# Leaving out a DMA that reads one element of each row of w_in ahead of its load

## The chip, the cores and the metric

The kernel runs on one core of a Trainium2 chip. The metric is the device time of one execution in microseconds (us), as the median of several runs. A core has five engines that run their own instruction lists in order: TensorE (PE: matmuls, with weight loads shown as PEld), VectorE (DVE), ScalarE (ACT), GpSimd (POOL) and SyncE (SP). ScalarE, SyncE and GpSimd also issue DMA transfers, which 16 DMA engines carry out. A transfer that changes the type (here float32 in memory to float16 on the chip) is issued by GpSimd.

## The reference

Two stages. First an attention over 4 batches, 8 heads, 768 positions and 64 dimensions per head, with a bias by distance, in which each position sees the first 8 positions and the 96 latest ones:

```python
scores = scale * np.matmul(q, k.transpose(0, 1, 3, 2))
keep = is_global | is_local          # pos < 8, or 0 <= rel < 96
scores = np.where(keep, scores + bias, -1e9)
a = softmax(scores)
attn_out = np.matmul(a, v)
```

Its output, as 3072 tokens of 512 numbers, goes through two dense layers:

```python
h = np.maximum(x @ w_in, 0.0)        # w_in: 512 x 2048
out = (h * h) @ w_out                # w_out: 2048 x 512
```

## The kernel before

The 3072 tokens are cut into 24 tiles of 128; 6 tiles make a batch. Attention goes tile by tile: q and k are transposed (tile `trp`, L416, and a copy to `qk` by VectorE, L429), scores are computed against the tile itself and the one before (`sp`, L466), ScalarE takes the exponential (`ex`, L479), VectorE multiplies by a mask that holds bias and reach (`ph`, L485), TensorE multiplies with v (`av`, L495), VectorE divides (`rec`, `tm`, L504 and L505), and the result is transposed (`trx`, L511) into `xt`. From tile 6 on the transposes are done by DMA, issued by SyncE. `fix_k` and `fix_v` copy the first 32 positions of a batch from tile to tile.

The dense layers work on chunks of tiles, eight chunks of one tile and then eight of two. Layer 1 (`first`, L639) makes `hps` from `w_in_sb` and `xt` in 16 blocks of 128 of d_ff, with 4 matmuls for each block and chunk; ScalarE applies the maximum (`hr`, L647) and VectorE squares (`h`, L654). Layer 2 (`second`, L660) makes `yps` from `w_out_sb` and `h`, VectorE copies it, and SyncE stores it.

w_in is loaded in four quarters of 512 columns (`load_w_in`, L395), each with all 512 rows; w_out in four quarters of 512 rows (`load_w_out`, L402). All these loads, and those of q, k and v from tile 1 on (and v of tile 0), are issued by GpSimd in one written order (L728): v of tile 0; q, k, v of tiles 1 and 2; the first quarter of w_in; q, k, v of tile 3; the other three quarters of w_in; the four of w_out; then tiles 4 and up. q and k of tile 0 come by another way, as float32 in two halves each (`load_early`, L374): q on SyncE's queue, k on ScalarE's. Ahead of the k halves stands `touch_w_in` (L391): a DMA that reads the first element of each of w_in's 512 rows into a small tile that nothing uses.

The order of the rest is not written out: the class `Plan` makes it while the program is built. Each piece of work is added with an estimate of its length, with what it needs and makes, with buffers that it takes and frees, and a rank. `emit` then walks in planned time, picks for each engine what can start first, and by rank among those, and appends it to that engine's list. DMA transfers have an amount of work and share the DMA engines in the plan; a landing of GpSimd's loads comes later by `late(at)` nanoseconds, depending on the planned time. Where TensorE is planned to idle before 45 us, `idle` puts in matmuls on a blank tile (`warm`, L269), one for every 220 ns of the gap; their results are not used. What the chip does then follows the lists, and semaphores between engines, whatever the plan's times were. A change of an estimate or the loss of one DMA can therefore change the lists of all engines.

Of the kernel before, what the change touches and what calls it, by code (L numbers as in the profile page):

```python
# [8 lines left out]
FP32 = mybir.dt.float32  # L9
# [4 lines left out]
P = 128  # L14


class Dma:
# [5 lines left out]
    def add(self, at, queue, work, item):  # L23
        self.coming.append((at, queue, work, item))
        self.coming.sort(key=lambda x: x[0])
# [26 lines left out]
class Plan:  # L52
# [115 lines left out]
                gone[key] = done  # L168

    def late(self, at):  # L170
        return 700 if at < 15500 else 1300 if at < 43000 else 0


SURE = {"PE": 0, "ACT": 60, "DVE": 60}
# [4 lines left out]
def kernel(  # L179
# [11 lines left out]
    nc = tc.nc  # L191
# [3 lines left out]
    d_model, d_ff = moe_w_in.shape  # L195
    NT = S // P
    NPAIR = H // 2
    NFT = d_ff // P
    NCT = d_model // P
# [12 lines left out]

    NUDGE = {('attention', 11): -10, ('attention', 1): 10, ('attention', 13): -10, ('attention', 7): 100, ('layer 2', 1): 25, ('layer 2', 6): 100, ('attention', 8): 10, ('layer 2', 11): -100, ('attention', 3): 10, ('layer 1', 9): -100, (3.5, 1): 100, ('attention', 20): -25, (2.5, 2): 200, (2, 9): -100, ('attention', 6): 10, (4.5, 16): 25, ('layer 2', 13): -200, ('attention', 23): -200, (1.5, 4): -25, ('layer 1', 5): -10, ('layer 1', 10): -10, ('attention', 5): -200, (4, 16): -100, ('layer 2', 0): 50, ('attention', 19): -10, (2, 4): 25, ('attention', 14): 200, ('attention', 9): 50, ('layer 1', 1): 100, (2, 15): -10, (6, 11): -10, ('attention', 18): -10, ('layer 2', 15): 10, ('attention', 2): -100, ('layer 1', 0): 50, (1.5, 8): 100, (3, 3): 200, ('layer 1', 11): -50, (6, 4): 10, ('layer 1', 2): -25, ('layer 2', 8): 50, ('attention', 10): 25, (1.5, 9): 100, (4.5, 4): -10, ('layer 1', 8): 10, (4.5, 7): 100, ('layer 1', 14): 100, ('layer 1', 13): -25}

    EARLY_QK, TOUCH = ("SP","ACT"), "ACT"

    EARLY_V = None

    W_IN = 4


    ADDED = 0
# [11 lines left out]
    const = ctx.enter_context(tc.tile_pool(name="const", bufs=1))  # L234
# [18 lines left out]

    mask = const.tile([P, 3, 2, NPAIR, P], FP16, name="mask")
    w_in_sb = const.tile([P, NCT, d_ff], FP16, name="w_in_sb")
    touched = const.tile([P, NCT, 1], FP32, name="touched")
    w_out_sb = const.tile([P, NFT, d_model], FP16, name="w_out_sb")


# [14 lines left out]
    add = plan.op  # L274
    vec = nc.vector
    live = {}

    def pool_dma(ns, fn, work, **how):
        add("POOL", ns, fn, work=work, to=914, back=850, **how)
# [42 lines left out]
    def constants():  # L322
        add("DVE", 120, lambda: vec.memset(blank, 0.0), rank=-999)
        add("DVE", 250, lambda: vec.tensor_scalar(
            out=ident, in0=dist[:, 0:P], scalar1=0.0, scalar2=None, op0=ALU.is_equal),
            needs=["dist"], makes=["ident"], rank=-999)
        if EARLY:
            add("DVE", 250, lambda: vec.tensor_scalar(
                out=ident32, in0=dist[:, 0:P], scalar1=0.0, scalar2=None, op0=ALU.is_equal),
                needs=["dist"], makes=["ident32"], rank=-998)  # L330
        add("DVE", 2350, fill_reach, needs=["dist"], makes=["reach"], rank=-997)
        if ADDED:
            for h in range(H):
                add("ACT", 190, lambda h=h: fill_diag(h), needs=["ident"], makes=[("diag", h)],
                    rank=-990 + h)
        for h in range(H):
            add("ACT", 420, lambda h=h: fill_mask(h), needs=["reach"], makes=[("mask", h)],
                rank=-990 + h if h < 4 else -185)
# [22 lines left out]
    def fetch(t, names="qkv"):  # L361
        for name in names:
            pool_dma(876, lambda name=name: load(t, name), 851, makes=[("s" + name, t)],
                     takes=[("stage", ("stage", t))] if name == "q" else
                     [("v", ("v", t))] if name == "v" else [],
                     needs=["ones"] if name == "v" else [])
# [20 lines left out]
            needs=["ev", "ones"], makes=[("sv", 0)], takes=[("v", ("v", 0))], rank=-100)  # L387


    def touch_w_in():  # L390
        {"ACT": nc.scalar, "SP": nc.sync}[TOUCH].dma_start(out=touched, in_=moe_w_in[:, 0:1].rearrange("(k p) f -> p k f", p=P))  # L391

    def load_w_in(c):
        n = d_ff // W_IN
        pool_dma(745, lambda: nc.gpsimd.dma_start(  # L395
            out=w_in_sb[:, :, c * n:(c + 1) * n],
            in_=moe_w_in[:, c * n:(c + 1) * n].rearrange("(k p) f -> p k f", p=P)),
            10240 // W_IN if W_IN == 4 else 1340, makes=[("w_in", c)])

    def load_w_out(c):  # L400
        n = NFT // 4
# [124 lines left out]
    def all_of(name, t):  # L526
        return [(name, t, p) for p in parts_of(t)]
# [95 lines left out]
    def banks(t0):  # L623
        return 1 if t0 < 12 else 2

    def home(t0):
        return "one" if t0 in (0,) else "big"

    def first(c, t0, n, m):
        per = 4 // n  # L630
        if m == 0:
            live["h2", c] = buf("h2", [P, NFT * 2 * P], FP16, "h2")[:, 0:NFT * n * P].rearrange(
                "p (m c) -> p m c", m=NFT)
        i, place = divmod(m, banks(t0) * per)
        if place == 0:
            live["hps", c, i] = buf(home(t0), [P, banks(t0), 512], FP32, "hps")
        w, o = divmod(place, per)
        for kk in range(NCT):
            nc.tensor.matmul(live["hps", c, i][:, w, o * n * P:(o + 1) * n * P],  # L639
                             lhsT=w_in_sb[:, kk, m * P:(m + 1) * P],  # L640
                             rhs=live["xt", c][:, kk, 0:n * P],
                             start=kk == 0, stop=kk == NCT - 1)

    def relu(c, t0, n, i):
        live["hr", c, i] = hr = buf("hr", [P, 2, 512], FP16, "hr")
        w, x = 4 // n * n * P, banks(t0)
        nc.scalar.activation(out=hr[:, 0:x, 0:w], in_=live["hps", c, i][:, 0:x, 0:w], func=AF.Relu)  # L647

    def square(c, t0, n, i):
        per, x = 4 // n, banks(t0)  # L650
        hr = live["hr", c, i][:, 0:x, 0:per * n * P]
        to = live["h2", c][:, x * per * i:x * per * (i + 1), :].rearrange(
            "p (x m) c -> p x (m c)", x=x)
        vec.tensor_tensor(out=to, in0=hr, in1=hr, op=ALU.mult)  # L654
# [17 lines left out]
    def layer_1(c, t0, n, due):  # L672
        xs = [y for t in range(t0, t0 + n) for y in all_of("x", t)]
        per, x = 4 // n, banks(t0)
        for m in range(NFT):
            i, place = divmod(m, x * per)
            add("PE", 4 * (n * 54 + 1), lambda m=m: first(c, t0, n, m),
                needs=xs + [("w_in", m * W_IN // NFT)] + ([("l1", c, m - 1)] if m else []),
                makes=[("l1", c, m)],
                takes=([(home(t0), ("hps", c, i))] if place == 0 else [])  # L680
                + ([("h2", ("h2", c))] if m == 0 else []),
                frees=[("xt", c)] if m == NFT - 1 else [], rank=due(m))
            if place == x * per - 1:
                cols = x * per * n * P
                add("ACT", 70 + 84 * cols // 100, lambda i=i: relu(c, t0, n, i),
                    needs=[("l1", c, m)], makes=[("hr", c, i)], frees=[("hps", c, i)],
                    takes=[("hr", ("hr", c, i))], rank=due(m))
                add("DVE", 90 + 52 * cols // 100, lambda i=i: square(c, t0, n, i),
                    needs=[("hr", c, i)], makes=[("h2", c, y) for y in range(
                        x * per * i, x * per * (i + 1))], frees=[("hr", c, i)], rank=due(m))  # L690
# [25 lines left out]
    with tc.manual_schedule():  # L716
        for names, t in []:
            fetch(t, names)
        add("POOL", 470, iota, makes=["dist"])
        constants()  # L720
        add("DVE", 300, ones, makes=["ones"], rank=-995)
        if EARLY:
            fetch_early()
        if EARLY_V:
            fetch_early_v()
        if TOUCH:
            add(TOUCH, 530, touch_w_in, rank=-1000, work=460, to=210, back=1000)
        for kind, n in [('v', 0), ('qkv', 1), ('qkv', 2), ('i', 0), ('qkv', 3), ('i', 1), ('i', 2), ('i', 3), ('o', 0), ('o', 1), ('o', 2), ('o', 3), ('qkv', 4), ('qkv', 5), ('qkv', 6), ('qkv', 7), ('qkv', 8), ('qkv', 9), ('qkv', 10), ('qkv', 11), ('qkv', 12), ('qkv', 13), ('qkv', 14), ('qkv', 15), ('qkv', 16), ('qkv', 17), ('qkv', 18), ('qkv', 19), ('qkv', 20), ('qkv', 21), ('qkv', 22), ('qkv', 23)]:  # L728
            if kind in "io":
                {"i": load_w_in, "o": load_w_out}[kind](n)  # L730
            else:
                fetch(n, kind)
        t0 = 0
        for c, n in enumerate(CHUNKS):
            for j in range(n):
                attention(t0 + j, c, j, n, lambda st, t0=t0, j=j, n=n:
                          100 * (t0 - n + j) + 6 * st - 100
                          + NUDGE.get(("attention", t0 + j), 0) + NUDGE.get((st, t0 + j), 0))
            layer_1(c, t0, n, lambda m, t0=t0, n=n, c=c: 100 * (t0 + n * m / NFT)
                    + NUDGE.get(("layer 1", c), 0))  # L740
            layer_2(c, t0, n, lambda j, part, t0=t0, n=n, c=c: 100 * (t0 + n + j + part / 4)
                    + 150 + NUDGE.get(("layer 2", c), 0))
            t0 += n
        plan.emit()
# [35 lines left out]
```

## Time and profile before

| | |
|---|---|
| Median of 3 runs | 215.76 us (215.57 to 215.81) |
| The profiled execution's own time | 214.87 us |
| Its span | 213.1 us |
| TensorE busy | 205.6 us, 96% of the span |
| VectorE, ScalarE, GpSimd busy | 122.1, 102.7, 68.1 us |
| Layer 1, layer 2 matmuls | 91.7 and 91.2 us busy |
| Granted TensorE clock | 0.998 |

The span is the part of one execution that the profiler saw from the first to the last instruction; the execution's own time lies 1.77 us above it. In the chain, every line is a stretch of work that released the next one, back from the end. In the timeline, the first number is the start, the second the length, and what stands in square brackets is the idle time before it, with what ended it. A DMA's landing is counted from its issue.

### The profile page before, as it was taken

The page shows a single profiled execution, that of the slowest core. Times are in us where ns is not written, and L with a number is a line of the kernel's source. Part 1 is how long each engine was busy: PE and PEld are TensorE (multiplying, and loading weights), DVE is VectorE, ACT ScalarE, POOL GpSimd, SP SyncE. Part 2 cuts the span into 40 slices and gives each one's busy share as a digit, 9 for nine tenths or more (in the row PEclk, how much of TensorE's full clock was granted, in tenths as well). Part 3 has the DMA queues.
Part 4 walks back from the last instruction along what each step waited for, and adds up shares of the span by engine and source line. Part 5 has one row for each costly group of instructions (what it writes and reads, how often), then busy time and mean ns, then how long its engine had stood idle before and what let it go on. Part 6 is the DMA issues. An engine that isn't in the chain of part 4 may idle for free.

```text
span 213.1 us, 5399 instructions
## 1 busy us (share of the span) xinstructions
PE 205.6 (96%) x2253; PEld 145.6 (68%) x2253; DVE 122.1 (57%) x296; ACT 102.7 (48%) x132; POOL 68.1 (32%) x84
## 2 busy tenths in 40 slices
PE   7869999999999999999999999999999999999994
PEld 4458986657967665875878585757676574888453
DVE  5697562774647877657566545664646674232321
ACT  4775663433764656565464635453353641345100
POOL 8975433727604544632207230451000000000000
PEclk9999999999999999999999999999999999999999
DMA  8999999999996999999939999699511222100112
GB/s 121 150 174 205 207 207 173 182 150 253 154 166 127 163 185 203 183 136 205 173 67 98 137 127 134 115 148 179 105 25 52 77 69 82 49 0 3 49 49 98
DMA packets 112232, 27.61 MB, mean 130 GB/s; under 512 B 104784, under 2 KB 109264, under 8 KB 112208
## 3 DMA queue, kind: packets, MB, share of 16 engines
q0 software_dynamic: 77024, 13.37, 87.3%
q1 hardware_dynamic: 33600, 13.64, 30.7%
q10 hardware_dynamic: 1584, 0.26, 0.7%
q8 instruction: 17, 0.28, 0.5%
q14 instruction: 7, 0.06, 0.1%
HBM read 27.27 MB, written 6.29 MB: 157 GB/s over the span
## 4 chain that ended last, share of the span: by engine, by line
PE 90%; DMA 4%; POOL 3%; DVE 1%; issue 0%
PE yps L660 40%; PE hps L639 39%; PE sp L466 5%; PE av L495 5%; DMA w_in_sb<-in_moe_w_in_dram 4%; POOL s L359 2%; POOL v L359 1%; PE trp L416 1%; PE trx L511 0%; DVE qk L429 0%; DVE tm L505 0%; PE warm L269 0%; DVE rec L504 0%; DVE y L429 0%; DVE v L442 0%
## 5 line engine op out<-in xcount | busy, mean ns | idle before, releaser
L639 PE MATMUL hps<-xt,w_in_sb 128*128 128x128 f16 (+1 forms) x1024 | 91.7, 246 | 1.0 <-DMA w_in_sb<-in_moe_w_in_dram 1.0
L660 PE MATMUL yps<-w_out_sb,h 128*128 128x512 f16 (+2 forms) x416 | 91.2, 363 | 0.0
L639 PEld LDWEIGHTS <-w_in_sb 128*128 128x128 f16 x1024 | 79.2, 98 | 12.7 <-DMA w_in_sb<-in_moe_w_in_dram 1.2
L647 ACT ACTIVATE hr<-hps 128x512 f16<-128x512 f32 (+1 forms) x72 | 52.7, 739 | 68.5 <-PE hps L639 64.9
L660 PEld LDWEIGHTS <-h 128*128 128x128 f16 x416 | 37.0, 98 | 34.8 <-DVE h L654 0.4
L654 DVE TENSOR_TENSOR h<-hr 128x512 f16<-128x512 f16 (+1 forms) x72 | 36.7, 511 | 38.8 <-ACT hr L647 38.6
L479 ACT ACTIVATE ex<-sp 128x1024 f16<-128x1024 f32 (+1 forms) x45 | 42.9, 1002 | 20.0 <-PE sp L466 19.9
L359 POOL DMA_DIRECT2D v<-in_v_dram x24 | 21.5, 896 | 64.1 <-issue 19.7
L485 DVE TENSOR_TENSOR ph<-ex,mask 128x1024 f16<-128x1024 f16 (+1 forms) x45 | 30.0, 676 | 14.1 <-ACT ex L479 13.9
L429 DVE COPY y<-yps 128x512 f32<-128x512 f32 (+2 forms) x26 | 16.9, 648 | 20.0 <-PE yps L660 19.7
L359 POOL DMA_DIRECT2D s<-in_q_dram x23 | 20.5, 891 | 7.9 <-PE hps L639 2.4
L359 POOL DMA_DIRECT2D s<-in_k_dram x23 | 20.7, 898 | 4.6 <-DMA w_out_sb<-in_moe_w_out_dram 2.9
L505 DVE TENSOR_TENSOR tm<-av,rec 128x256 f16<-128x256 f32 x48 | 20.4, 424 | 1.7
L495 PE MATMUL av<-v,ph 128*128 128x65 f16 x352 | 15.0, 193 | 1.0 <-DVE ph L485 1.0
L466 PEld LDWEIGHTS <-qk 64*128 64x128 f16 x352 | 9.9, 94 | 8.7 <-issue 5.9
L495 PEld LDWEIGHTS <-ph 128*128 128x128 f16 x352 | 13.6, 97 | 3.1 <-DVE ph L485 1.4
L466 PE MATMUL sp<-qk 64*128 64x128 f16 x352 | 14.2, 218 | 0.5 <-DVE qk L429 0.2
L504 DVE RECIPROCAL rec<-av 128x4 f32<-128x4 f32 x48 | 8.5, 176 | 9.3 <-PE av L495 9.2
L269 PE MATMUL warm<-blank 128*128 128x256 f16 x37 | 7.7, 317 | 1.2 <-DVE v L345 1.2
L439 DVE COPY qk<-qk 128x128 f16<-128x128 f16 x16 | 4.8, 302 | 1.2 <-PE sp L466 0.6
L427 ACT COPY xt<-trx 128x512 f16<-128x512 f16 (+1 forms) x6 | 3.1, 515 | 4.9 <-PE trx L511 4.9
L269 PEld LDWEIGHTS <-blank 128*128 128x128 f16 x37 | 3.8, 113 | 2.1 <-DVE v L345 1.2
(32 smaller groups left out, 38.1 us busy)
## 6 DMA issues: line engine op xcount, KB each, us to landing
out_dram<-y SPq DMA_DIRECT2D x23, 256.0 KB, 3.4
v<-in_v_dram POOLq DMA_DIRECT2D x24, 128.0 KB, 5.0
s<-in_q_dram POOLq DMA_DIRECT2D x23, 128.0 KB, 5.3
s<-in_k_dram POOLq DMA_DIRECT2D x23, 128.0 KB, 5.9
w_in_sb<-in_moe_w_in_dram POOLq DMA_DIRECT2D x4, 512.0 KB, 10.1
w_out_sb<-in_moe_w_out_dram POOLq DMA_DIRECT2D x4, 512.0 KB, 15.9
qk<-s SPq DMA_TRANSPOSE x18, 6.0
xt<-tm SPq DMA_TRANSPOSE x18, 4.6
```

Of the source, the lines that this page charges most:

```text
L269: nc.tensor.matmul(to[:, 0:2 * P], lhsT=blank[:, 0:P], rhs=blank[:, 0:2 * P], start=True, stop=True)
L359: nc.gpsimd.dma_start(out=dst, in_=source(t, name))
L429: vec.tensor_copy(out=out, in_=src)
L466: nc.tensor.matmul(live["sp", t, before, part][:, e, a, :], lhsT=live["qk", t - before][rows, 1, a, :], rhs=live["qk", t][rows, 0, a, :], ...
L479: nc.scalar.activation(out=some(live["ph" if t < ADDED else "ex", t, before], part), in_=some(live["sp", t, before, part], part), func=AF. ...
L485: vec.tensor_tensor(out=some(live["ph", t, before], part), in0=some(live["ex", t, before], part), in1=some(mask[:, kind], part), op=ALU.mult)
L495: nc.tensor.matmul(av[:, i, :], lhsT=live["ph", t, before][:, h % 2, h // 2, :], rhs=v_bufs[(t - before) % len(v_bufs)][:, h, :], start=be ...
L505: vec.tensor_tensor(out=live["tm", t][:, 4 * g:4 * g + 4, :], in0=av[:, :, 0:D], in1=rec[:, :, None].to_broadcast([P, 4, D]), op=ALU.mult)
L639: nc.tensor.matmul(live["hps", c, i][:, w, o * n * P:(o + 1) * n * P], lhsT=w_in_sb[:, kk, m * P:(m + 1) * P], rhs=live["xt", c][:, kk, 0: ...
L647: nc.scalar.activation(out=hr[:, 0:x, 0:w], in_=live["hps", c, i][:, 0:x, 0:w], func=AF.Relu)
L654: vec.tensor_tensor(out=to, in0=hr, in1=hr, op=ALU.mult)
L660: nc.tensor.matmul(live["y", c, j, cols][:, 0:cols[1] - cols[0]], lhsT=live["h2", c][:, m, j * P:(j + 1) * P], rhs=w_out_sb[:, m, cols[0]: ...
```

## The change

The call of `touch_w_in` falls away, with its tile, so that ScalarE's list begins with the two k halves of tile 0. The function itself is written anew, but with `TOUCH = ()` nothing calls it. The width of w_in's parts is given as a list of four equal ones, which is the same four quarters with the same planned work. And `late` changes: between 11.5 and 15.5 us of planned time, GpSimd's loads are now taken to land 1300 ns late instead of 700. `NUDGE`, which shifts ranks, is unchanged.

```diff
     def late(self, at):
-        return 700 if at < 15500 else 1300 if at < 43000 else 0
+        return 700 if at < 11500 else 1300 if at < 43000 else 0
...
-    EARLY_QK, TOUCH = ("SP","ACT"), "ACT"
+    EARLY_QK = ("SP","ACT")
+    TOUCH = ()
...
-    W_IN = 4
+    W_IN = (4,) * 4
...
-    touched = const.tile([P, NCT, 1], FP32, name="touched")
...
-    def touch_w_in():
-        {"ACT": nc.scalar, "SP": nc.sync}[TOUCH].dma_start(out=touched, in_=moe_w_in[:, 0:1].rearrange("(k p) f -> p k f", p=P))
+    def touch_w_in(queue, behind):
+        to = const.tile([P, NCT, 1], FP32, name="touched")
+        if behind:
+
+            add("DVE", 60, lambda: vec.memset(to, 0.0), needs=behind, makes=["touch"], rank=-1000)
+        add(queue, 530, lambda: {"ACT": nc.scalar, "SP": nc.sync}[queue].dma_start(
+            out=to, in_=moe_w_in[:, 0:1].rearrange("(k p) f -> p k f", p=P)),
+            needs=["touch"] if behind else [], rank=-1000, work=460, to=210, back=1000)
 
     def load_w_in(c):
-        n = d_ff // W_IN
+        at = slice(sum(W_IN[:c]) * P, sum(W_IN[:c + 1]) * P)
         pool_dma(745, lambda: nc.gpsimd.dma_start(
-            out=w_in_sb[:, :, c * n:(c + 1) * n],
-            in_=moe_w_in[:, c * n:(c + 1) * n].rearrange("(k p) f -> p k f", p=P)),
-            10240 // W_IN if W_IN == 4 else 1340, makes=[("w_in", c)])
+            out=w_in_sb[:, :, at], in_=moe_w_in[:, at].rearrange("(k p) f -> p k f", p=P)),
+            200 + 590 * W_IN[c], makes=[("w_in", c)])
...
-                needs=xs + [("w_in", m * W_IN // NFT)] + ([("l1", c, m - 1)] if m else []),
+                needs=xs + [("w_in", [c for c, n in enumerate(W_IN) for _ in range(n)][m])] + ([("l1", c, m - 1)] if m else []),
...
-        if TOUCH:
-            add(TOUCH, 530, touch_w_in, rank=-1000, work=460, to=210, back=1000)
+        for queue, behind in TOUCH:
+            touch_w_in(queue, behind)
```

## The prediction

> **What bounds the kernel now.** I read the engines in stretches of the span first, then the chain that ended last, and then the landings of the loads in the first 30 us. The stretches (columns: length; busy time and instructions of PE, weight loads, DVE, ACT, POOL; granted clock; DMA share; GB/s):
>
> ```profile
> span 213.1 us, 5399 instructions
> 15.28:20.36 5.08, 4.87 (x86) 4.16 (x87) 4.50 (x13) 2.04 (x4) 3.11 (x4) 1.00 1.42 201
> 20.36:60.00 39.64, 39.64 (x547) 30.48 (x548) 22.68 (x54) 20.83 (x32) 19.27 (x22) 1.00 1.82 189
> 60.00:150.00 90.00, 90.00 (x987) 63.04 (x988) 57.30 (x140) 47.71 (x58) 32.45 (x37) 1.00 1.54 150
> 150.00:209.99 59.99, 59.98 (x522) 40.82 (x516) 26.78 (x55) 21.86 (x22) 0.00 (x0) 1.00 0.18 54
> ```
>
> From 20.36 us to 209.99 us TensorE has no gap and keeps a clock of 1.00. The time is therefore the moment at which this dense stretch begins, plus a fixed amount of matmul work, plus a short tail. A change at the head counts one to one if it moves that moment, and not at all otherwise. The chain (start, length, piece) shows how TensorE gets there:
>
> ```profile
> 7.72 7.51 DMA w_in_sb<-in_moe_w_in_dram
> ...
> 16.57 0.22 PE warm L269 x2
> ...
> 17.34 0.26 PE av L495 x8
> ...
> 19.00 0.61 DVE qk L429
> ...
> 19.66 0.62 PE sp L466 x16
> ...
> 20.49 7.19 PE hps L639 x128
> 27.68 0.48 PE av L495 x16
> 28.17 1.56 PE hps L639 x28
> 29.73 0.36 PE trx L511 x4
> 30.09 0.22 PE hps L639 x4
> 30.31 0.86 PE yps L660 x4
> ```
>
> The last gate is found by adding landing to issue. The first four rows are single transfers (us from issue to landing): v of tile 2, the first quarter of w_in, v of tile 3, the second quarter; below them are their issues from the timeline, and the weight loads that start the dense stretch:
>
> ```profile
> v<-in_v_dram POOLq DMA_DIRECT2D x1, 128.0 KB, 5.0
> w_in_sb<-in_moe_w_in_dram POOLq DMA_DIRECT2D x1, 512.0 KB, 7.5
> v<-in_v_dram POOLq DMA_DIRECT2D x1, 128.0 KB, 7.7
> w_in_sb<-in_moe_w_in_dram POOLq DMA_DIRECT2D x1, 512.0 KB, 9.3
> ...
> 6.85 0.92 POOL L359 DMA_DIRECT2D v<-in_v_dram  x1
> 7.72 0.81 POOL L395 DMA_DIRECT2D w_in_sb<-in_moe_w_in_dram  x1
> 10.20 0.96 POOL L359 DMA_DIRECT2D v<-in_v_dram  x1
> 11.06 2.32 POOL L395 DMA_DIRECT2D w_in_sb<-in_moe_w_in_dram  x3
> 20.36 5.70 PEld L639 LDWEIGHTS <-w_in_sb 128*128 128x128 f16 x102
> ```
>
> 11.06 + 9.3 = 20.36: the second quarter lands just as the dense matmuls start. The scores of tile 3 ended shortly before (19.66 + 0.62 = 20.28). Two gates lie within 0.1 us, and the later one is a landing. The four landings are 11.85, 15.23 (7.72 + 7.51), 17.9 and 20.36. So the first quarter took 3.38 us behind the transfer ahead of it, and the second 2.46 us for the same bytes: 0.9 us more, with the touch in place.
>
> **Part 1, the touch goes.** It is one issue on ScalarE's queue and 512 packets of 4 bytes on the 16 DMA engines. The first rows are of the queues in the first 5 us (packets, MB, time in packets as a share of 16 engines); the last is of v's transfers between 100 and 150 us:
>
> ```profile
> q10 hardware_dynamic: 1583, 0.26, 31.0%
> q1 hardware_dynamic: 1056, 0.26, 23.2%
> 0.74 0.48 ACTq L391 DMA_DIRECT2D touched<-in_moe_w_in_dram  x1
> 1.25 1.16 ACTq L374 DMA_DIRECT2D early<-in_k_dram  x2
> 2.00:3.00 1.00, 1.00 (x7) 0.73 (x5) 0.93 (x6) 0.56 (x1) 1.00 (x2) 1.00 1.05 174
> 5.00:7.00 2.00, 1.76 (x16) 0.92 (x16) 1.33 (x2) 1.58 (x4) 2.00 (x4) 1.00 2.33 148
> DMA to landing us min/median/max: 3.9/4.6/4.9
> ```
>
> q10 is ScalarE's queue (the k halves and the touch), q1 is SP's (the q halves, the same bytes as k). The difference is the touch: (31.0% - 23.2%) x 5 us = 0.39 us of all 16 engines. It moves w_in only if the DMA engines, not POOL's issuing, set the pace of the loads. The DMA share is over 1 from 2 us on, and v of tile 2 needs 5.0 us to land where a late v needs 3.9 at best: some 1.1 us of waiting lies ahead of POOL's loads, more than is taken away. So the engines set the pace, and both quarters of w_in land 0.39 us earlier, at 14.84 and 19.97. The ends of this price: nothing, if the issues set the pace after all, and 0.51 us (1.25 - 0.74), the step that k moves up in ScalarE's queue. I take 0.39, which is the work itself.
>
> The Trainium skill (DMA: Bandwidth & Descriptors, "Issuing engines are not separate DMA queues") speaks against the larger end: transfers issued by different engines run on the same 16 DMA engines and interleave, so an earlier issue saves sequencer time alone. By that rule the queue place buys nothing beyond the work removed; by the place alone the sum below would be 0.12 us lower.
>
> **Part 2, w_in's first quarter now reads rows that nothing has read.** No row shows this, so it is bounded by neighbours. The nearest weights that nothing touched are w_out's (the last quarter of w_in, the first two of w_out, and when the last w_in issue began):
>
> ```profile
> w_in_sb<-in_moe_w_in_dram POOLq DMA_DIRECT2D x1, 512.0 KB, 12.8
> w_out_sb<-in_moe_w_out_dram POOLq DMA_DIRECT2D x1, 512.0 KB, 14.7
> w_out_sb<-in_moe_w_out_dram POOLq DMA_DIRECT2D x1, 512.0 KB, 15.0
> ...
> L395 POOL DMA_DIRECT2D w_in_sb<-in_moe_w_in_dram x4: 809/840/847, 7.7 to 12.5; - x4
> 13.27 0.86 POOL L402 DMA_DIRECT2D w_out_sb<-in_moe_w_out_dram  x1
> 15.52 1.58 POOL L402 DMA_DIRECT2D w_out_sb<-in_moe_w_out_dram  x2 [1.39 <-DMA w_in_sb<-in_moe_w_in_dram]
> ```
>
> Landings: 25.3, 27.97, 30.52. The untouched first quarter of w_out takes 2.67 us, the next 2.55: reading fresh rows costs 0.1 us there. The other row is w_in's own 0.9 us excess: it stands in spite of the touch, so the touch does not prevent it. The ends are therefore 0.9 us won (the excess goes, should the touch cause it) and 0.9 us lost (a second one). I take zero, nearest to w_out's 0.1, since the excess with the touch says nothing for the touch.
>
> The Trainium skill (the same page, "Latency and other measured facts") says that DMA engines 7 and 15 are usually slower than the others, with a best guess at contention around the descriptor rings of GpSimd's loads. By that rule part of the excess belongs to engines, not to rows, and stays as it is; the view of landings shows no single engine, so no row here tests it.
>
> **Part 3, the planner's changed lateness and the new order.** The built program's lists show what moves. On TensorE all of tile 0 to 2's work ahead of w_in is the same, but the four k transposes come together. Behind w_in's landing come 8 matmuls of layer 1, the 4 transposes of tile 1's x, 8 of layer 1, 2 warm ones, then av of tile 2 in two halves with 4 of layer 1 between, and only then tile 3's transposes, 12 of layer 1, 4 transposes, 2 warm and tile 3's scores. The length of this path, to the scores' end, from rows above: layer 1 at 0.056 us (7.19 / 128) x 20 = 1.1; 4 transposes 0.36; 2 warm 0.22; av 0.48: 2.2 us; then DVE must divide and free tile 2, and copy qk of tile 3, which in the chain takes from 17.60 (17.34 + 0.26, av's end) to 19.61 (19.00 + 0.61), that is 2.0 us; scores 0.6. Sum 4.8 us. From 14.84 the scores end at 19.6, and the landing at 19.97 stays the gate, with 0.3 us to spare.
>
> Behind the gate: 16 matmuls of layer 1, **one warm matmul that was not there**, 64, av, 28, 4 transposes, 20, and the first group of w_out. Before, the warm ones all lay ahead of the gate. This one is inside the dense stretch and costs 0.11 us (0.22 / 2). The first use of w_out comes 32 matmuls of layer 1 earlier (160 before it in the old list, 128 in the new one): 32 x 0.056 = 1.8 us, so 30.31 - 1.8 + 0.1 = 28.6 in the old time, against a landing of 27.97: 0.6 us of cover, which falls away if w_out lands late relative to the second quarter of w_in.
>
> ScalarE does 4 masks, then tile 0's exponentials, then 4 masks (6 and 2 before); the first six and VectorE's masking of tile 2's weights in the old timeline:
>
> ```profile
> 3.99 2.59 ACT L316 ACTIVATE mask<-reach 128x384 f16<-128x384 f16 x6 [0.27 <-DVE reach L308]
> 15.23 1.28 DVE L485 TENSOR_TENSOR ph<-ex,mask 128x1024 f16<-128x1024 f16 x2
> ```
>
> Nothing behind the two moved masks ends later than w_in's landing; that wait is their cover, and without it they cost 0.9 us (2 x 2.59 / 6). On VectorE tile 3's division comes after 4 squares, not 7; PE has other work there. POOL's list is the same. On SP a transpose of qk goes ahead of one store of out; it sits in the dense stretch and costs nothing while no TensorE wait is seen there. From some 40 us on all lists agree.
>
> **Sum.** -0.39 (DMA work) + 0 (fresh rows) + 0.11 (warm) = -0.28 us. The profiled execution took 214.87 us, 1.77 around its span of 213.1, and would take 214.59. The median of the runs is 215.76, 0.89 above it. I apply the difference there: 215.5 us.
>
> **Rivals.**
> A, slower: the touch did warm w_in's rows, and without it the first quarter stalls again by 0.9 us. Loads of POOL's queue land in order, so the second quarter shifts as well, and so does the gate: -0.39 + 0.9 + 0.11 = +0.62, 216.4 us. For it: only w_in's first pass has an excess, the later three have none. Against it: w_out's 0.1 us. It decides from 0.28 us of extra stall on.
> B, much faster: the excess is made by the touch, or falls away by chance of order. The second quarter could land at 19.1; tile 2's DVE work then becomes the bound, because its masked weights, ready at 16.51 before, come some 0.4 us earlier, at 16.1: then av and 4 matmuls of layer 1 (0.7), division and copy (2.0), scores (0.6), so 19.4. Gain 20.36 - 19.4 - 0.1 = 0.9, 214.9 us. Nothing in the profile ties the excess to the touch, which was issued 7 us ahead of that load.
> C, the change is hidden: POOL's issues, one per 0.87 us, set the pace, the landings stay, and the new order costs its warm matmul or a wait for w_out: +0.1 to +0.4, 215.9 us. Against it: the 1.1 us of waiting ahead of the loads.
>
> **How the numbers follow.** What lies within 0.2% (0.43 us) can hardly be told from no change. Forecast 0.40: its spread of -0.7 to +0.1 us puts 0.16 into faster and 0.24 into the same (its own range 215.0 to 215.9). A 0.37: 0.35 slower, 0.02 the same. B 0.15, faster. C 0.08: 0.04 the same, 0.04 slower. Together faster 0.31, same 0.30, slower 0.39. The range goes from 214.8 (B) to 216.7 (A with a stall of 1.2 us).
>
> **What would show it.** Touch row gone; the early k halves landing 0.4 us or more earlier; w_in's quarters landing near 14.8 and 20.0; the dense stretch from 20.0 without a wait, one warm matmul after its first 16. Wrong if w_in's first quarter lands after 15.3 (A), before 14.3 (B), or if TensorE waits behind 20 us (C).

## The result, and the profile after

Without the touch the kernel takes 217.48 us (median of 22 runs, 215.01 to 221.58) against 215.71 us for the kernel before (22 runs on the same chip, 214.55 to 217.06). The ratio is 1.0061, with a 95% interval of 1.0038 to 1.0085: the change makes the kernel slower, by some 1.3 us. The ratio leaves out, as slow, five runs of this kernel, of 218.51 us and more; with them the medians lie 1.77 us apart. The forecast was 215.5 us and its range ended at 216.7.

The profiled execution took 216.96 us, with a span of 215.2 us; before, these were 214.87 and 213.1. Its four stretches, cut as before the change (length; busy time and instructions of PE, weight loads, DVE, ACT, POOL; granted clock; DMA share; GB/s):

```profile
span 215.2 us, 5398 instructions
15.30:20.39 5.09, 4.63 (x84) 3.98 (x84) 4.36 (x13) 2.10 (x4) 3.12 (x4) 1.00 1.40 201
20.39:60.00 39.61, 39.24 (x544) 30.52 (x545) 22.14 (x53) 20.55 (x32) 19.28 (x22) 1.00 1.77 182
60.00:150.00 90.00, 88.77 (x969) 62.16 (x968) 56.60 (x138) 47.08 (x59) 32.44 (x37) 1.00 1.52 150
150.00:211.93 61.93, 61.93 (x536) 41.77 (x534) 27.74 (x56) 22.86 (x23) 0.00 (x0) 1.00 0.22 57
```

Before, TensorE had no gap from 20.36 us on. Now 0.37 us are missing in the second stretch (39.61 - 39.24) and 1.23 us in the third. What TensorE waited for there, from the view of waits behind 20.5 us (us in total, times, longest):

```profile
PE hps L644 <- DMA xt<-tm: 1.2, 1, 1.2
PE hps L644 <- DMA w_in_sb<-in_moe_w_in_dram: 0.4, 1, 0.4
```

The timeline of after gives the places (start, length, in brackets the idle time before it):

```profile
6.87 0.92 POOL L359 DMA_DIRECT2D v<-in_v_dram  x1
7.73 0.80 POOL L401 DMA_DIRECT2D w_in_sb<-in_moe_w_in_dram  x1
11.09 2.32 POOL L401 DMA_DIRECT2D w_in_sb<-in_moe_w_in_dram  x3
19.63 0.62 PE L471 MATMUL sp<-qk 64*128 64x128 f16 x16
20.39 0.90 PEld L644 LDWEIGHTS <-w_in_sb 128*128 128x128 f16 x16 [0.32 <-DMA w_in_sb<-in_moe_w_in_dram]
21.30 0.27 PE L269 MATMUL warm<-blank 128*128 128x256 f16 x1
25.99 1.74 PE L644 MATMUL hps<-xt,w_in_sb 128*128 128x128 f16 x28 [0.36 <-DMA w_in_sb<-in_moe_w_in_dram]
64.19 1.07 PE L644 MATMUL hps<-xt,w_in_sb 128*128 128x128 f16 x16 [1.24 <-DMA xt<-tm]
```

The chain that ended last carries the same two places as DMA pieces, which the dense stretch of before did not have:

```profile
12.57 13.38 DMA w_in_sb<-in_moe_w_in_dram
...
25.99 1.74 PE hps L644 x28
...
56.26 7.88 DMA xt<-tm
...
64.19 1.07 PE hps L644 x16
```

And the landings of single loads, from their issue: v of tile 2, the first quarter of w_in, v of tile 3, the second quarter:

```profile
v<-in_v_dram POOLq DMA_DIRECT2D x1, 128.0 KB, 5.1
w_in_sb<-in_moe_w_in_dram POOLq DMA_DIRECT2D x1, 512.0 KB, 7.5
v<-in_v_dram POOLq DMA_DIRECT2D x1, 128.0 KB, 7.7
w_in_sb<-in_moe_w_in_dram POOLq DMA_DIRECT2D x1, 512.0 KB, 9.3
```

The second quarter lands at 11.09 + 9.3 = 20.39 us, against 20.36 before. The head gained nothing. The k halves did land sooner, at 4.74 us (issued at 0.74, 4.0 us to landing) against 5.05 (1.25 and 3.8), but the q halves, issued at 0.74 in both, took 3.5 us against 2.9. The account of this one execution, for 2.1 us more span: the start of the dense stretch +0.03, the warm matmul inside it +0.11 (the prediction's price), the wait for w_in's last quarter +0.36, the wait for x of tile 6 +1.24: together 1.74. Nearly 0.4 us are left: 0.2 more of busy time behind 20.39 us beside the warm matmul, and 0.16 behind TensorE's last matmul. How much of this belongs to the change, and how much to this one execution, is what the experiments had to tell, since the times of one kernel lie 2 us and more apart from run to run.

### The profile page after: what moved, and what is told of

It is laid out like the page before. It is cut to its first block, busy times and chain, and to the rows that moved or that the text cites. A ratio compares the mean times of both kernels' runs of the same rounds, so it can differ in the third digit from the quotient of the medians.

```text
span 215.2 us, 5398 instructions
## 1 busy us (share of the span) xinstructions
PE 206.1 (96%) x2254; PEld 146.2 (68%) x2254; DVE 121.8 (57%) x296; ACT 102.8 (48%) x132; POOL 68.1 (32%) x84
## 4 chain that ended last, share of the span: by engine, by line
PE 83%; DMA 10%; POOL 5%; DVE 0%; issue 0%; ACT 0%
PE yps L665 38%; PE hps L644 35%; DMA w_in_sb<-in_moe_w_in_dram 6%; PE sp L471 5%; PE av L500 4%; DMA xt<-tm 4%; POOL s L359 2%; POOL v L359 2%; POOL w_in_sb L401 1%; PE trp L421 0%; PE trx L516 0%; DVE y L434 0%; DVE blank L323 0%; DVE v L345 0%; ACT hr L652 0%
## 5 line engine op out<-in xcount | busy, mean ns | idle before, releaser
L484 ACT ACTIVATE ex<-sp 128x1024 f16<-128x1024 f32 (+1 forms) x45 | 42.9, 1002 | 20.7 <-PE sp L471 20.5
L359 POOL DMA_DIRECT2D v<-in_v_dram x24 | 21.5, 896 | 63.1 <-issue 19.6
```

What stands on the lines that cost most here:

```text
L359: nc.gpsimd.dma_start(out=dst, in_=source(t, name))
L484: nc.scalar.activation(out=some(live["ph" if t < ADDED else "ex", t, before], part), in_=some(live["sp", t, before, part], part), func=AF. ...
```

## The experiments

Any edit of the plan can move all lists. So each kernel but one (the exchange of two loads) carries the lists of TensorE, ScalarE, VectorE and SyncE and the places of the warm matmuls written out, taken from one of the two kernels. "Old lists" are those of before, "new lists" those of after. The old lists then stay as they are when the touch is added, taken out or aimed elsewhere. In the lists the touch is piece 18, the k halves are 15 and 17. In the expectations, the ratio is to the kernel before on the same chip. The touch feeds nothing in any of them.

**1. The touch alone, the lists alone.** Four kernels: the old lists without touch, the new lists with it, and SyncE's one exchange (positions 6 and 7: a store of out, and the transpose of qk of tile 8) undone or made alone.

```diff
# old lists, no touch            (TOUCH as in before: ScalarE, ahead of k)
-    TOUCH = (("ACT", ()),)
+    TOUCH = ()
# new lists, with touch
-    TOUCH = ()
+    TOUCH = (("ACT", ()),)
# new lists, no touch, SyncE's list of before
-    "SP": [14,16,145,369,190,408,235,451,280,
+    "SP": [14,16,145,369,190,408,451,235,280,
# old lists, touch, SyncE's list of after
-    "SP": [14,16,146,370,191,409,452,236,281,
+    "SP": [14,16,146,370,191,409,236,452,281,
```

> All engines follow the lists of the kernel before, instruction by instruction, and only the touch is left out. Theory O (the order made the loss, the touch's absence costs nothing): within 0.5 us of before, w_in's first quarter landing between 14.8 and 15.3 us. Rival T (the missing touch makes the loss, through later or more scattered landings): 217.0 us or more, about the loss of the whole change (1.8 us), and a landing of a w_in quarter later than before's 15.23 or 20.36.

> All engines follow the lists of the changed kernel, and the touch stands ahead of the k halves on ScalarE's queue as before. Theory O: 217.0 to 217.8 us, as slow as the changed kernel. Rival T: 215.4 to 216.2 us, as before.

> The changed kernel with one swap undone: on SyncE the store of out for chunk 1 stands ahead of the transpose of tile 8's qk again. Theory O with SyncE as its main part: the 1.2 us wait of layer 1 for x of tile 6 goes, and 215.9 to 216.4 us are left (the warm matmul of 0.1 and the wait for w_in's last quarter of 0.4). If the swap isn't the cause: 217.2 us or more, with the wait for x still there.

> The kernel before, touch and all, with that one swap made on SyncE. Theory O with SyncE as its main part: 216.5 to 217.3 us, with a wait of layer 1 for x of tile 6 of about 1 us. If the swap isn't the cause: 215.4 to 216.0 us.

Measured, as ratios: the old lists without touch 1.0037 (0.9998 to 1.0076); the new lists with touch 1.0010 (0.9975 to 1.0046); the new lists without touch and with SyncE's old order 1.0032 (1.0000 to 1.0064); the old lists with SyncE's new order 1.0037 (1.0000 to 1.0074). The larger part of the loss seemed to be the missing touch, against the prediction, which had put it at -0.39 us. By its median (215.89 us) the second kernel lies where rival T had put it; the first (216.36) lies between the two theories. SyncE's exchange was not settled. The medians of the last two kernels (216.19 and 216.99 us) lie where "SyncE as the main part" had put them, and undoing the exchange on the new lists saved 0.29% (1.0061 against 1.0032), about as much as making it on the old ones cost, 0.37%. Against it, the wait for x did not go when it was undone (two waits, 1.8 us in sum), and the new lists with touch contain it and cost 0.10%.

**2. Which rows, how many, and where in ScalarE's queue.** All with the old lists: the touch reads 512 rows of w_out instead of w_in; it reads 64 rows of w_in; it comes behind the two k halves; and the old lists without touch again.

```diff
# rows of w_out
-    out=to, in_=moe_w_in[:, 0:1].rearrange("(k p) f -> p k f", p=P)
+    out=to, in_=moe_w_out.rearrange("(r e) d -> r e d", e=4)[:, 0, 0:1].rearrange("(k p) f -> p k f", p=P)
# 64 rows
-    out=to, in_=moe_w_in[:, 0:1].rearrange("(k p) f -> p k f", p=P)
+    out=to[0:16], in_=moe_w_in.rearrange("(r e) f -> r e f", e=8)[:, 0, 0:1].rearrange("(k p) f -> p k f", p=16)
# behind k
-    "ACT": [18,15,17,
+    "ACT": [15,17,18,
```

> The lists of before; the same 512 packets of 4 bytes on ScalarE's queue, 8 KB apart as before, but from w_out and not from w_in. Theory W (the touch works by having read w_in's rows): as slow as without a touch, 216.2 to 217.0 us, w_in's first quarter landing at 15.5 us or later. Rival D (the touch works by its own packets, as a delay or by taking DMA time at the head): as before, 215.2 to 215.8 us, landing at 15.2 or earlier.

> The lists of before; only every eighth row of w_in is touched, 64 packets and not 512. If what is warmed covers 64 KB or more of w_in: as before, 215.2 to 215.8 us. If it is each row of 8 KB by itself: 7 of 8 rows stay cold and it is as slow as without a touch, 216.2 to 217.0 us.

> The lists of before, with the touch behind the two k halves on ScalarE's queue and not ahead of them. Theory W: it is still 5 us ahead of w_in's first quarter, so 215.1 to 215.8 us, as before. Rival D: the head is as without a touch, 216.2 us or more.

> The first experiment once more, beside the other three on the same chip: the lists of before without the touch. Theory W and rival D alike: 216.2 to 217.0 us. If it is within 0.3 us of before, the missing touch costs nothing with the old lists and the first experiment's 0.9 us was scatter.

On the chip of these four the kernel before took 216.10 us, so the times that were expected are read as ratios to it. Measured: w_out's rows 1.0012 (0.9978 to 1.0046), 64 rows 1.0005 (0.9973 to 1.0038), behind k 0.9979 (0.9955 to 1.0004), no touch again 1.0034 (1.0006 to 1.0062). The missing touch costs again, and this time the interval is clear of 1. A touch that never reads w_in lay between the two theories, with an interval that holds both, and was repeated below. Behind k, where it no longer delays k, the touch does as well.

**3. The first big load, whatever it carries.** The written order of GpSimd's loads is changed: the first quarter of w_out takes the place of the first of w_in, and the reverse. Nothing is touched; the planner makes its own lists.

```diff
-    ('qkv', 2), ('i', 0), ('qkv', 3), ('i', 1), ('i', 2), ('i', 3), ('o', 0),
+    ('qkv', 2), ('o', 0), ('qkv', 3), ('i', 1), ('i', 2), ('i', 3), ('i', 0),
```

> The changed kernel, without a touch, with the first quarters of w_out and w_in changing places in GpSimd's list: w_out's comes right after v of tile 2, w_in's last of the four. TensorE then waits longer for w_in; the time isn't the point (some 10 us more). What counts is how long each transfer takes behind the one ahead of it. Theory W (w_in's rows are cold): w_out's quarter passes in about 2.6 us in the first place, and the first w_in quarter to come (behind v of tile 3) takes 3.0 us or more. Rival P (the first transfer of 2 KB rows behind the small ones pays, whichever it is): w_out's takes 3.2 us or more there, and w_in's 2.5.

One execution, 225.26 us; the time is not of interest, since all of w_in now comes later. The landings (v of tile 2, the first quarter of w_out, v of tile 3, the first quarter of w_in that is loaded), issued at 6.87, 7.73, 10.22 and 11.09 us:

```profile
v<-in_v_dram POOLq DMA_DIRECT2D x1, 128.0 KB, 4.8
w_out_sb<-in_moe_w_out_dram POOLq DMA_DIRECT2D x1, 512.0 KB, 7.8
v<-in_v_dram POOLq DMA_DIRECT2D x1, 128.0 KB, 8.0
w_in_sb<-in_moe_w_in_dram POOLq DMA_DIRECT2D x1, 512.0 KB, 9.5
```

w_out's quarter takes 15.53 - 11.67 = 3.86 us behind the load ahead of it, and w_in's behind it 20.59 - 18.22 = 2.37 us. In this execution the long pass went with the place and not with the tensor, and fresh rows of w_in were read at the fast pace. It is a single execution, and the table below shows that the place of the long pass changes from one to the next.

**4. Repeats, and rows of neither weight.** The touch of w_out's rows and the touch behind k again, the new lists with touch again; then a touch of 512 rows of q, twice, 64 rows behind k, and the old lists without touch a third time.

```diff
# rows of q
-    out=to, in_=moe_w_in[:, 0:1].rearrange("(k p) f -> p k f", p=P)
+    out=to, in_=q.rearrange("b h s d -> (b h s) d").rearrange("(r e) d -> r e d", e=32)[0:512, 0, 0:1].rearrange("(k p) f -> p k f", p=P)
```

> The touch of w_out in place of w_in's, once more, since the first time lay between the two theories (1.0012, interval 0.9978 to 1.0046). Theory W: a ratio of 1.003 or more. Rival D: 1.001 or less.

> The lists of before with the touch behind the k halves, once more, since it was the fastest so far (0.9979, interval 0.9955 to 1.0004). If that holds: a ratio of 0.997 to 0.999. If it was scatter: 0.999 to 1.002.

> The changed kernel's lists with the touch, once more (1.0010 the first time, interval 0.9975 to 1.0046). If the new lists cost what is left of the loss beside the touch: a ratio of 1.0015 to 1.004. If they cost nothing: 0.999 to 1.001.

> The lists of before; the same 512 packets on ScalarE's queue, 8 KB apart, but from q, of which other transfers read parts anyway. Theory R (the two weights lie in one stretch of memory that is slow to be read first; touching either one helps, and without a touch the first big load pays, whichever it is): no help, so a ratio of 1.003 or more, the first quarter of w_in 7.6 us or more from issue to landing, under 183 GB/s between 10.5 and 13 us. Rival D (the packets help by themselves, wherever they read): a ratio of 1.001 or less, a landing at about 7.0 us, 190 GB/s.

> The lists of before with the smallest touch in the best place: 64 rows of w_in, behind the k halves. Theory R: as with any touch of weights, a ratio of 0.998 to 1.001. Rival D, by the number of packets: between before and no touch, 1.001 to 1.004.

> The lists of before without a touch, beside the touch of q on the same chip: a ratio of 1.0035, as in both earlier runs (1.0037 and 1.0034).

> The touch of q a second time, for the interval and for a second profile: as the first one of it, by either theory.

Measured: w_out's rows 0.9991 (0.9963 to 1.0019); behind k 1.0002 (0.9976 to 1.0027); new lists with touch 1.0015 (0.9989 to 1.0041); rows of q 0.9984 (0.9959 to 1.0009) and 0.9992 (0.9960 to 1.0024); 64 rows behind k 1.0052 (1.0025 to 1.0078); no touch for the third time 1.0018 (0.9984 to 1.0053). A touch of 512 rows of anything, ahead of k or behind it, gives the time of before in six measurements of six (0.9979 to 1.0012, mean 0.9993). No touch gives 1.0037, 1.0034 and 1.0018 (mean 1.0030). With q's rows the intervals end at 1.0009 and 1.0024, so the touch does not work by having read w_in's rows, nor those of either weight. 64 rows behind k were slower than either theory allowed. The halved loss of the third repeat shows how near this effect lies to what can be measured.

**5. Four rows, and 1024 rows.** What remained was the delay that the touch gives k, or its packets on the DMA engines. A touch of 4 rows ahead of k was meant to give the delay without the packets, one of 1024 rows (of w_out) twice the packets.

```diff
# 4 rows, to one partition
-    out=to, in_=moe_w_in[:, 0:1].rearrange("(k p) f -> p k f", p=P)
+    out=to[0:1], in_=moe_w_in.rearrange("(r e) f -> r e f", e=128)[:, 0, 0:1].rearrange("(k p) f -> p k f", p=1)
# 1024 rows
-    out=to, in_=moe_w_in[:, 0:1].rearrange("(k p) f -> p k f", p=P)
+    out=to, in_=moe_w_out.rearrange("(r e) d -> r e d", e=2)[:, 0, 0:1].rearrange("(k p) f -> p k f", p=P)
```

> Edit: before's lists replayed, and the touch, in its old place ahead of the k halves, reads 4 rows (one element each, to one partition) rather than 512. The issue on ScalarE's queue and the place of k behind it stay; nearly all its packets go. Theory D1 (what helps is that k comes 0.4 to 0.5 us later): ratio to before 0.998 to 1.002, first quarter of w_in from issue to landing near 7.1 us. Theory D2 (the packets on the DMA engines help): like no touch, ratio 1.002 to 1.005, first quarter near 7.8 us. The 64 rows ahead of k, at 1.0005, spoke for D1.

> Edit: before's lists replayed, and the touch, in its old place, reads the first element of 1024 rows of w_out: twice the packets. Theory D1 (the delay of k) and D2 (packets): k some 0.3 us later still and the loads of POOL later behind them; if the first quarter of w_in gains more by it, it lands no later than with 512 rows and the ratio is 0.997 to 1.001; if the gain is a step that 64 or 512 rows already give, the extra 0.3 to 0.4 us of DMA work is a plain loss: ratio 1.001 to 1.003. Either way the GB/s between 10.5 and 13 us should be at or above 190.

Measured: 4 rows 1.0043 (1.0013 to 1.0072), 1024 rows 1.0031 (0.9997 to 1.0065). The first test is not clean. The timeline of the kernel with 4 rows:

```profile
0.74 1.18 ACTq L386 DMA_DIRECT2D touched<-in_moe_w_in_dram  x1
1.97 0.96 ACTq L365 DMA_DIRECT2D early<-in_k_dram  x2
```

The issue to one partition took 1.18 us, where that of before took 0.48, so k was issued at 1.97 rather than 1.25 us: more delay than the touch ever gave. Its landings (v of tile 2, first quarter, v of tile 3, second quarter, issued at 6.87, 7.74, 10.22 and 11.09 us) bear on another reading:

```profile
v<-in_v_dram POOLq DMA_DIRECT2D x1, 128.0 KB, 4.8
w_in_sb<-in_moe_w_in_dram POOLq DMA_DIRECT2D x1, 512.0 KB, 6.3
v<-in_v_dram POOLq DMA_DIRECT2D x1, 128.0 KB, 6.5
w_in_sb<-in_moe_w_in_dram POOLq DMA_DIRECT2D x1, 512.0 KB, 9.1
```

The first quarter passes in 14.04 - 11.67 = 2.37 us, without any excess, and the second takes 20.19 - 16.72 = 3.47. The long pass has moved one load on, and the second quarter lands where it did. The dense stretch of this execution begins later all the same, behind tile 3's scores, after a stretch of low clock (last section):

```profile
20.88 0.62 PE L462 MATMUL sp<-qk 64*128 64x128 f16 x16 [0.20 <-DVE qk L425]
21.55 0.67 PE L635 MATMUL hps<-xt,w_in_sb 128*128 128x128 f16 x9
```

**All profiles together.** For each kernel the ratio, and from its one profiled execution: the first big load from issue to landing; the pass of the first and of the second big load (landing less the landing of the v ahead of it); when the second landed; and the sum of TensorE's waits for DMA inside the dense stretch, by the view of waits. Where a row is of two kernels with one program, their numbers stand side by side, passes with a semicolon between them.

| kernel | ratio | first load, us | passes, us | second lands | waits for DMA, us |
|---|---|---|---|---|---|
| before | 1 | 7.5 | 3.37, 2.46 | 20.36 | 0 |
| after | 1.0061 | 7.5 | 3.26, 2.47 | 20.39 | 1.6 |
| old lists, no touch (second, third) | 1.0034, 1.0018 | 7.3, 7.5 | 3.16, 2.06; 3.56, 2.37 | 20.07, 20.29 | 0.3, 0 |
| new lists with touch (twice) | 1.0010, 1.0015 | 6.9, 7.8 | 3.27, 2.46; 3.76, 2.47 | 19.76, 20.69 | 0, 0.3 |
| new lists, no touch, SyncE old | 1.0032 | 8.3 | 4.36, 2.46 | 21.16 | 1.8 |
| old lists, touch, SyncE new | 1.0037 | 7.4 | 3.27, 1.96 | 20.46 | 2.0 |
| rows of w_out (twice) | 1.0012, 0.9991 | 6.5, 7.4 | 2.46, 3.26; 3.26, 2.37 | 20.17, 20.19 | 0.3, 0 |
| rows of q (twice) | 0.9984, 0.9992 | 7.2, 7.4 | 3.56, 2.47; 3.57, 2.26 | 19.99, 20.16 | 1.8, 0.2 |
| behind k (twice) | 0.9979, 1.0002 | 6.9, 6.6 | 2.87, 1.96; 2.86, 2.67 | 19.86, 19.69 | 0.8, 1.6 |
| 64 rows ahead of k | 1.0005 | 6.5 | 2.46, 1.96 | 20.27 | 0 |
| 64 rows behind k | 1.0052 | 7.8 | 3.96, 2.37 | 20.59 | 0.9 |
| 4 rows ahead of k | 1.0043 | 6.3 | 2.37, 3.47 | 20.19 | 0 |
| 1024 rows of w_out | 1.0031 | 6.2 | 2.46, 3.16 | 19.76 | 0.2 |

The first profile of the old lists without touch is left out of the table, because its clock was low (0.50 from 16 to 19 us) and its span 219.2 us. Its loads were the latest of all, though: the first took 8.2 us, the passes were 4.06 and 2.46 us, and the second quarter landed at 22.06.

Two things are read from this table. First, in the stretch from v of tile 2 to the second quarter some excess is there in every kernel: its place changes (first load, second load, the load of q, k and v between them: 4.09 us with 64 rows ahead of k, where most show 2.69), with and without touch. Second, one profiled execution does not order the kernels. The kernel with 1024 rows has the second quarter 0.6 us earlier than before and is not faster; one of the two profiles of the touch of q has 1.8 us of waits and belongs to the kernels with the lowest medians. The wait for x of tile 6 is found with SyncE's old order too, as in that profile (waits of the kernel that touches q):

```profile
PE hps L635 <- DMA xt<-tm: 1.2, 1, 1.2
PE hps L635 <- DMA w_in_sb<-in_moe_w_in_dram: 0.6, 1, 0.6
```

And in the profile of the old lists with SyncE's new order:

```profile
PE hps L635 <- DMA xt<-tm: 2.0, 1, 2.0
```

It is missing in both profiles of the new lists with touch, which hold the exchange as well. SyncE's exchange is therefore neither needed for that wait nor sufficient for it; whether it makes it longer or more frequent, one profile of each kernel does not tell.

## Why the prediction was wrong, point by point

**What bounds the kernel: right up to one inference.** In after the gate is the second quarter's landing (20.39, with the scores ended at 19.63 + 0.62 = 20.25), as forecast. In before the two gates lay closer than the prediction's sum has it, because its chain runs from the scores through a warm matmul into the dense stretch (in the timeline the next matmuls overlap it from 20.36 us on), which the lines shown there leave out:

```profile
20.28 0.22 PE warm L269
```

With the old lists the quarter was there 0.17 us before the dense stretch began in one execution (rows of w_out, 20.17 and 20.34) and 0.28 in another (1024 rows, 19.76 and 20.04): there the scores were the gate. The inference that failed is another: "no gap from 20.36 us on" was read as if nothing in that stretch could gate. It is one execution without a wait. Of the 13 profiles of the table with SyncE's old order, the kernel before aside, nine have waits for w_in's last quarter or for an x (mostly of tile 6, in two of them of a later tile near 145 us), 0.2 to 1.8 us in sum. How much slack there was can be worked out. SyncE's timeline of before, around the transpose of x of tile 6 (issued at 55.72):

```profile
45.89 1.63 SPq L422 DMA_TRANSPOSE qk<-s  x1
47.84 0.34 SPq L670 DMA_DIRECT2D out_dram<-y  x1
49.44 1.24 SPq L422 DMA_TRANSPOSE qk<-s  x1
53.19 0.34 SPq L670 DMA_DIRECT2D out_dram<-y  x1
55.72 1.19 SPq L523 DMA_TRANSPOSE xt<-tm  x1
```

Tile `tm` of before from 45 to 68 us, where x of tile 6 is the slowest:

```profile
DMA to landing us min/median/max: 4.6/5.2/5.8
```

So it landed at 55.72 + 5.8 = 61.5 us. The chain of before has the 16 matmuls that use it at 62.41:

```profile
62.41 0.89 PE hps L639 x16
```

That is about 0.9 us of slack, not an unlimited one. SyncE's timeline of after, where a store of out waits behind the transpose of tile 8's qk, two stores go together, and x follows them:

```profile
45.77 5.71 SPq L427 DMA_TRANSPOSE qk<-s  x2
51.57 2.49 SPq L675 DMA_DIRECT2D out_dram<-y  x2
56.26 1.20 SPq L528 DMA_TRANSPOSE xt<-tm  x1
```

Tile `tm` of after, in the same stretch:

```profile
DMA to landing us min/median/max: 7.9/7.9/7.9
```

In after x was there at 64.14 (56.26 + 7.88 in the chain) and could have been used at 64.19 - 1.24 = 62.95. The same transpose scatters by far more than the slack: in the 14 profiles of the table with SyncE's old order it takes 5.2 to 8.1 us to land, in the four with the new order 6.2 to 8.6.

**Part 1, the touch's DMA work: the step that failed.** It said that both quarters of w_in land 0.39 us earlier, because the DMA engines set the pace. They land where they did (15.23 and 20.39; forecast 14.84 and 19.97). The work removed was also smaller. The queues of after in the first 5 us (packets, MB, share of 16 engines), q10 now with the k halves alone and q1 with the q halves:

```profile
q10 hardware_dynamic: 1056, 0.26, 25.9%
q1 hardware_dynamic: 1056, 0.26, 23.4%
```

(31.0% - 25.9%) x 5 us = 0.26 us; q was not a true stand-in for k. And that 0.26 us did not reach the loads: v of tile 2 lands 5.1 us after its issue, against 5.0 with the touch. The 1.1 us that I had read as waiting for engines is there without the touch. On the old lists the two quarters landed without the touch at 15.92 and 22.06, 15.02 and 20.07, 15.23 and 20.29 us in three executions: no steady gain there either. The lower end of the range of this step, "nothing", was the right one, and half of rival C was right with it. Its condition, "if the issues set the pace after all", is not shown: the landings stay 5 us behind the issues either way. The prediction's own rows left room for this end: the DMA share was 2.33 at 148 GB/s from 5 to 7 us and 1.42 at 201 GB/s from 15.28 us on, so the larger share carried less, and a share above 1 is no measure of what the engines could still take. The Trainium skill (DMA: Bandwidth & Descriptors, "Issuing engines are not separate DMA queues") says that transfers started by different engines share the same 16 DMA engines, and that starting them from several engines saves only the time to start them. The runs don't contradict it: k's issue came at 0.74 instead of 1.25 us, and no load of GpSimd's queue between v of tile 2 and the second quarter of w_in landed sooner.

**Part 2, fresh rows at no cost: no sign against it, but wrong as a sum.** Fresh rows cost nothing that shows: w_in's rows pass in 2.37 us when w_out goes first, and a touch of q or w_out does as well as one of w_in. The 0.9 us excess is not tied to the tensor. Yet the touch was not free to remove. On unchanged lists, Parts 1 and 2 together were forecast at -0.39 us; the three measurements 1.0037, 1.0034 and 1.0018 make it +0.8, +0.7 and +0.4 us at 215.4 to 216.1 us. So the sign was wrong. Rival A had the sign, and its 216.4 us came nearer to the result than the forecast, but its mechanism, warmed rows of w_in, does not fit the touches of w_out and q. The Trainium skill's remark on slower DMA engines 7 and 15 (DMA: Bandwidth & Descriptors, "Latency and other measured facts") was tested by no run here.

**Part 3, the new order: its size is not settled.** It was to cost 0.11 us. The new lists with touch measure 1.0010 and 1.0015, 0.2 to 0.3 us, with intervals that hold both that and zero. The warm matmul is where it was forecast (21.30, behind the first 16 matmuls), and the path to tile 3's scores ended at 20.25, not 19.6, because the first quarter's landing, where it starts, hadn't moved: from 15.23 it took 5.0 us, against 4.8 in the sum. The wait for w_in's last quarter (0.36 us) was not foreseen: covers were counted for w_out alone. That quarter landed at 25.3 in before, by the prediction's own rows, and in after TensorE was ready for it at 25.63 (25.99 - 0.36), so its cover was thin. "SP's exchange costs nothing" is neither shown nor refuted.

The parts add up to the result within their intervals: about +0.3% for the touch (the mean of three is 0.30%), about +0.1% for the lists (mean of two 0.13%), against 0.61% (0.38 to 0.85). Another split fits as well: +0.3% for the touch and +0.3% for SyncE's exchange (0.37% alone on the old lists, 0.29% between 1.0061 and 1.0032 on the new ones), with nothing for the rest of the lists. The new lists with touch, at 0.10 and 0.15%, speak against it, but their intervals reach 0.46 and 0.41%. The touch's share is about the same in both; what the exchange costs stays open.

**What stays open.** Why a touch of 512 rows helps at all. It isn't the rows, the tensor, the memory region or its place ahead of k, and no single profile shows the 0.3% as one wait in one place. It isn't the small tile that it fills either: the kernels with 4 rows and with 64 rows behind k have that tile and lose time (1.0043 and 1.0052). The second quarter landed at 20.13 us on average in the ten profiles with a touch of 512 rows (19.69 to 20.69) and at 20.48 in the four of the table without one (20.07 to 21.16). That is a hint at most, since the ranges overlap and neither 4 rows (20.19) nor 1024 rows (19.76) follow it. That its packets keep the DMA engines at the head a little further behind GpSimd's issues, and that later loads then stumble less, would fit 64 rows behind k (1.0052) and 512 rows (0.9979 to 1.0012), but 64 rows ahead of k (1.0005) and 1024 rows (1.0031) speak against "more is better", and the test with 4 rows changed the delay too. This reading is not shown. A delay of k without any DMA was not tried, but behind k the touch helps without delaying it. The granted clock isn't it: among the executions of the old lists without touch, leaving out those with a mean clock under 0.996 leaves medians 0.74, 0.75 and 0.48 us above those of before, treated alike.

None of the kernels beats the kernel before by more than its interval: the touch of q (0.9984, 0.9992) and the touch behind k (0.9979, 1.0002) come nearest.

## What to carry to other kernels

A profile without a wait shows one execution: before putting an edit at nothing because "no wait is seen there", work out when the data landed and when it was needed, and compare that slack (here 0.9 us) with the spread of the transfers (here 5.2 to 8.1 us for the same transpose, issued in the same order). Removing DMA work pays only if the next landing moves; check first whether it would, and don't credit the removed work to loads that are issued 7 us later. Where an edit changes the planner's lists as well, write the lists out and change one thing at a time, and repeat the measurement before believing 0.3%.

## What the runs showed of the hardware that was not expected

- Among GpSimd's loads between 11 and 20 us, 512 KB mostly passes in 2.4 us (2.37 to 2.47; 1.96 behind a late v), and in every profile of the table one of the loads takes 0.5 to 2.0 us longer. The place varies between executions of the same program text: 2.46 and 3.26 us for the first and second big load in one profile of the touch of w_out's rows, and 3.26 and 2.37 in the other.
- A touch of 4 elements to one partition took 1.18 us to issue on ScalarE's queue, one of 64 elements to 16 partitions 0.44 us, one of 512 elements to 128 partitions 0.48 us.
- In the profile of the kernel with 4 rows, the granted clock fell to half for two us and more near 10 us, with TensorE busy 0.44 to 0.76 of each us from 6 to 10 us before it (columns as above):

```profile
6.00:7.00 1.00, 0.44 (x4) 0.27 (x3) 0.46 (x1) 0.84 (x3) 1.00 (x3) 1.00 2.33 149
9.00:10.00 1.00, 0.72 (x9) 0.72 (x10) 0.47 (x3) 1.00 (x3) 1.00 (x2) 0.61 2.43 155
10.00:11.00 1.00, 1.00 (x10) 0.84 (x8) 0.79 (x2) 0.08 (x2) 1.00 (x2) 0.50 2.25 165
```

Before has a busy share of 0.63 to 0.82 from 6 to 10 us and a clock of 1.00 throughout. What made the clock fall is not shown. The dense stretch of this execution began at 21.55 us, against 20.36 in before. This execution took 216.0 us, inside its kernel's spread (median 216.40).
